# Two steps moved in a fused attention and feed-forward kernel: the last batch's state rows, and four units of the second product

## The chip, the cores and the metric

The kernel runs on one core of a Trainium2 chip. The metric is the device time of one execution in microseconds (us). A core has TensorE (PE, matmuls; its weight loads are shown as PEld), VectorE (DVE), ScalarE (ACT), GpSimd (POOL) and SyncE (SP, which here only issues DMAs). Each engine works through its own list of instructions in order, and waits for another engine by semaphores.

## The reference

Attention between 8 batches of 512 rows and 32 state rows, 8 heads of 64, in both directions, and then a two-layer network with a leaky relu over the joined 4352 rows:

```python
scores = scale * x @ state.T ; a = softmax(scores) ; xread = a @ state      # 512 rows a batch
scores2 = scale * state @ x.T ; a2 = softmax(scores2) ; sread = a2 @ x      # 32 state rows a batch
attn = concatenate([xread, sread], axis=2)                                  # (8, 8, 544, 64)
x = attn.transpose(0, 2, 1, 3).reshape(8 * 544, 512)
h = x @ w_in          # 512 -> 2048
g = maximum(0.01 * h, h)
out = g @ w_out       # 2048 -> 512
```

## The kernel before

All data are held in bf16 for the products and summed in fp32. Order within each engine is the order in which the program was written: nothing is rescheduled.

For a batch's 512 rows the first product is rearranged: xread is never formed. Instead M = state times w_in (by heads) is computed (`a_m`, matmuls at L368, into the tile `pm`), copied out of PSUM by `m_evict` or by the copies at L1188 and L1166, and h = a times M is made in 16 steps s, each of two matmuls of 512 columns into a bank `ph` (`ff1`, L389). ACT applies the leaky relu, from `ph` to `hT` (L394). There are two `ph` banks.

The second product of a batch is done by a scheme with seven products in place of eight, numbered n = 1, 2, 6, 5, 7, 3, 4, over sums of parts of h (`su`, L655) and of w_out (`tw`). It is split into units (n, m), m from 0 to 7, each of two matmuls of 256 columns into `yq` (L666). n = 1, 6, 7, 4 add into one bank, n = 2, 5, 3 into the other. After n's last unit ACT saves the bank (`sv`, L675) or DVE adds it to a saved one (`yo`, L678).

The loop over batches b = 2 to 7 has 16 steps. In each, `ff1` makes a row of h, and `fill(s)` or `units(n)` runs a number of units: first those left of the batch before, then the first 15 of this batch itself (`OWN`). How many at which step stands in `PACE`, and for batch 2, whose first ten steps are taken by the second half of batch 1's rows (`half.run(7)`), in `PACE2`. In step 10, the three column blocks of the next batch's M are computed one after the other (called M's session here): `pm0` in the PSUM tile named big, `pm1` in the one named sc (which held the scores that the exponent `a_exp2`, L287, reads), `pm2` in the two `ph` banks. Then DVE and ACT copy `pm2` (L1188), and ACT copies `pm0` (L382). Step 10's `fill` stands ahead of M's session. Step 11's stands behind it and ahead of step 11's `ff1`; from step 12 on it stands behind the step's `ff1` again.

In the last batch (b = 7) there is no next one, and steps 4 to 11 do the first product by the seven-product scheme too (`FastLast`, two halves r of seven products, L552, tile `pl`). Products 1, 6, 7, 4 of a half share one bank, 2, 5, 3 the other. ACT saves products 1, 6 and 7 (L565), DVE saves 5 (L568), and DVE joins 2 and 3 with saved ones (L571); POOL adds 7 to 5 (L574). Relus follow (L559), some of them held back until the next save (`flush`). The second half runs in steps 8 to 11: products 1 and 2, then 6 and 5, then 7 and 3, then 4, with two units behind each product (four behind product 4).

The 32 state rows of each batch are read by `a_sread_rows` for batches 0 to 6. For batch 7 `a_sread` does it: 16 matmuls of 64 columns into `psr` (L315, in the tile big), and two copies by ACT into `sr_t` (L322). `sr_t` is read by `x_sums` on DVE (L445, in step 13) and by the state rows' own first product (`FastIn`, L463), which follows the loop.

Of the kernel before, what the change touches and what calls it, by code (L numbers as in the profile page):

```python
# [27 lines left out]
def kernel(  # L28
# [68 lines left out]
    def load_x(b, eng):  # L97
        xl[b] = xpool.tile([P, H, NT * D], FP32, name="xl", tag="xl", bufs=1)
        eng.dma_start(xl[b][:], x[b].rearrange("h (p t) d -> p h (t d)", t=NT))
# [103 lines left out]
    def a_scores(a):  # L203
        sc = psum.tile([P, 2, S], FP32, name="sc", tag="sc", bufs=1)
        for k in range(NK):
            for g in range(2):
                nc.tensor.matmul(  # L207
                    sc[NS * k:NS * (k + 1), g, :],
                    lhsT=st_of(a, g, k),
                    rhs=a.xT[D * g:D * (g + 1), :, k, :],  # L210
                    start=True, stop=True,
                )
        a.sc = sc
# [46 lines left out]
    def a_shift(a, part=None):  # L260
        flat = a.sc[:].rearrange("p g c -> p (g c)")
        if part != 1:
            a.mb = block_rows(block_max(flat, NB), NB)
        if part != 0:
            a.sh = block_sub(flat, a.mb, NB)
# [38 lines left out]
    def a_a2t(a):  # L304
        a.a2T = att.tile([P, 2, NT, P], BF16, name="a2T", tag="a2T", bufs=3)
        nc.sync.dma_start_transpose(
            a.a2T[:].rearrange("p g i q -> p (g i) q"),
            (a.a2 if a.b == B - 1 else a.e2)[:].rearrange("p g s -> p (g s)"),
        )

    def a_sread(a):
        ps = psum.tile([P, NK, 2, NS], FP32, name="psr", tag="big", bufs=1)
        for k in range(NK):
            for i in range(NT):
                nc.tensor.matmul(  # L315
                    ps[:, k, :, :],
                    lhsT=a.xb[:, i, 2 * k:2 * k + 2, :].rearrange("p h d -> p (h d)"),
                    rhs=a.a2T[:, :, i, NS * k:NS * (k + 1)],
                    start=(i == 0), stop=(i == NT - 1),
                )  # L320
        for g in range(2):
            nc.scalar.copy(  # L322
                sr_t[D * g:D * (g + 1), a.b], ps[D * g:D * (g + 1), :, g, :],
            )
# [51 lines left out]
    def m_evict(a, c, pm, copy):  # L376
        cols = slice(DM * c, DM * (c + 1))
        if isinstance(pm, list):
            for g in range(2):
                copy(a.M[:, g, cols], pm[g][:])  # L380
        else:
            copy(a.M[:, :, cols], pm[:])  # L382
# [3 lines left out]
    def ff1(a, hT, j):  # L386
        ph = psum.tile([P, S], FP32, name="ph", tag="ph")
        for g in range(2):
            nc.tensor.matmul(  # L389
                ph[:], lhsT=a.M[:, g, P * j:P * (j + 1)],  # L390
                rhs=a.aT[:, g, :],
                start=(g == 0), stop=(g == 1),
            )
        nc.scalar.activation(out=hT[:, j, :], in_=ph[:], func=AF.Prelu, alpha=0.01)  # L394
# [368 lines left out]

    OWN = 15
    PACE = (1, 4, 4, 4, 3, 4, 4, 3, 4, 4, 4, 4, 3, 4, 3, 3)
    PACE2 = (0,) * 10 + (3, 3, 2, 2, 2, 3)

    att_of = [Attn() for _ in range(B)]
    a0, a1, a2 = att_of[:3]
# [290 lines left out]
    for b in range(2, B):  # L1060
        hT = hpool.tile([P, 16, S], BF16, name="hT", tag="hT")
        a = att_of[b]
        nxt = att_of[b + 1] if b + 1 < B else None
        now = Batch(b, hT)
        std = []
        if b == 2:
            std = [(i, 3) for i in range(2)]
            for n in (0, 1):
                half.f.sums(n)

        def fill(s):
            units((PACE2 if b == 2 else PACE)[s])

        def units(n):
            left = min(n, len(before.units)) if before else 0
            if left:
                before.run(left)
            if n > left:
                now.run(n - left)

        for s in range(16):
            fast = nxt is None and 4 <= s < 12
            if fast:
                n = 1 if s in (7, 11) else 2
                k = PACE[s]
                for i in range(n):
                    fl.product()
                    units((i + 1) * k // n - i * k // n)
            elif s == 11:
                fill(s)  # L1090
            if not fast:
                ff1(a, hT, 4 + s if nxt is None and s < 4 else s)
            if s == 0:
                if b + 2 < B:
                    load_x(b + 2, nc.sync)
                a_a2t(a)
                if before:
                    for n in (0, 1):
                        before.f.sums(n, 4, 8)
            elif s == 1:  # L1100
                if nxt is not None:
                    a_scores(nxt)
                m_evict(a, 3, a_m(a, 3, "big"), SCA)
                if b == 2:
                    a_sread_rows([a0])
                elif b % 2:
                    a_sread_rows([att_of[b - 2], att_of[b - 1]])
                if b == 2:
                    half.f.sums(2)
                    a_shift(nxt, 0)  # L1110
                elif nxt is not None:
                    a_shift(nxt)
                if b + 2 < B:
                    open_xb(b + 2)
                    for h in range(0, H, 2):
                        cast_x(b + 2, h, h + 2, POO)
                if before:
                    before.f.sums(2, 4, 8)
            elif s == 3:
                if before:  # L1120
                    before.f.sums(3)
                if nxt is not None and b > 2:
                    a_max2(nxt)
            elif s == 4:
                if b == 2:
                    state_t(1)
                elif b == 4:
                    sread_t(0, 3)
                elif b == 7:
                    sread_t(1, 4)  # L1130
            elif s == 8:
                if nxt is None:
                    a_sread(a)
            elif s == 12:
                for n in range(3):
                    now.f.sums(n, 0, 4)
            if nxt is None:
                if s == 1:
                    fl = FastLast(a, hT)
                    fl.sums()  # L1140
                elif s in (6, 10):
                    fi.w_sum({6: 1, 10: 3}[s])
                elif s == 13:
                    fl.flush()
                    fi.x_sums()
            elif b >= B - 3 and s == 14:
                if b == B - 3:
                    fi = FastIn(None)
                fi.w_sum(2 * (b - (B - 3)))
            if s == (9 if b == 2 else 7) and b + 2 < B:  # L1150
                a_open(att_of[b + 2], b + 2)
                a_xt_dma(att_of[b + 2])
            if nxt is not None:
                if b == 2 and s < 11:
                    if s in (8, 9):
                        a_exp2(nxt, s - 8)
                elif s == 5:
                    a_exp(nxt)
                elif s in (7, 8):
                    a_exp2(nxt, s - 7)  # L1160
                    if s == 7:
                        a_probs(nxt)
                elif s == 11:
                    a_probs2(nxt)
                elif s in (12, 13):
                    SCA(nxt.M[:, s - 12, DM:2 * DM], pm1[:, s - 12, :])  # L1166
            if std:
                i, jq = std.pop(0)
                piece(1, h1, i, jq)
            elif b == 2 and half.units:  # L1170
                half.run(7)
                if s == 4:
                    a_shift(nxt, 1)
                    half.f.sums(3)
                    weights_sum(3)
                    a_max2(nxt)
                elif s == 6:
                    a_exp(nxt)
                elif s == 8:
                    a_probs(nxt, 0)  # L1180
            elif s != 11 and not fast:
                fill(s)
            if s == 10 and nxt is not None:
                pm0 = a_m(nxt, 0, "big")
                pm1 = a_m(nxt, 1, "sc")
                pm2 = a_m(nxt, 2, "ph")
                for g, copy in enumerate((VEC, SCA)):
                    copy(nxt.M[:, g, 2 * DM:3 * DM], pm2[g][:])  # L1188
                m_evict(nxt, 0, pm0, SCA)
                if b == 2:  # L1190
                    a_probs(nxt, 1)
        before = now
# [90 lines left out]
```

## Time and profile before

| | us |
|---|---|
| median of 3 runs | 203.49 (203.1 to 204.0) |
| profiled execution, its own time | 203.36 |
| its span, first to last instruction | 201.6 |
| PE busy | 195.9 (97%) |
| DVE busy | 159.5 (79%) |
| ACT busy | 145.0 (72%) |
| POOL busy | 42.6 (21%) |

The granted TensorE clock is 1.00 over the span. Busy times on PE come from modelled ends of matmuls: consecutive matmuls overlap in the record, so small waits between them do not show as idle time there. They show in the starts, from one matmul to the next, and in the chain of waits, where a piece's length is the time until the next piece. In a timeline row the columns are start, length, engine, line, operation, out<-in and shapes, and the number of instructions merged; the brackets give idle time before it and who ended it. The rows of M's session in batch 2's stretch lie at 66.3 to 67.1 us, those of the last batch's steps 8 to 11 at 166.3 to 172.1 us.

### The profile page before, as it was taken

The page shows a single profiled execution, that of the slowest core. Times are in us where ns is not written, and L with a number is a line of the kernel's source. Part 1 is how long each engine was busy: PE and PEld are TensorE (multiplying, and loading weights), DVE is VectorE, ACT ScalarE, POOL GpSimd, SP SyncE. Part 2 cuts the span into 40 slices and gives each one's busy share as a digit, 9 for nine tenths or more (in the row PEclk, how much of TensorE's full clock was granted, in tenths as well). Part 3 has the DMA queues.
Part 4 walks back from the last instruction along what each step waited for, and adds up shares of the span by engine and source line. Part 5 has one row for each costly group of instructions (what it writes and reads, how often), then busy time and mean ns, then how long its engine had stood idle before and what let it go on. Part 6 is the DMA issues. An engine that isn't in the chain of part 4 may idle for free.

```text
span 201.6 us, 4848 instructions
## 1 busy us (share of the span) xinstructions
PE 195.9 (97%) x2000; PEld 129.2 (64%) x2000; DVE 159.5 (79%) x241; ACT 145.0 (72%) x267; POOL 42.6 (21%) x69
## 2 busy tenths in 40 slices
PE   7899999999999999999999999999999999999993
PEld 2543444444377567766776677676767688799882
DVE  1676679899989889985997599779978977995612
ACT  3459839589869886978697868787878768767710
POOL 8931002021009005200410040200020014104250
PEclk9999999999999999999999999999999999999999
DMA  6999995999794995549343945250029101310035
GB/s 198 218 206 277 232 301 99 133 311 238 131 210 127 123 282 96 104 167 274 81 78 124 281 75 99 107 156 5 0 86 173 31 3 66 142 55 3 0 90 170
DMA packets 39733, 27.99 MB, mean 139 GB/s; under 512 B 25312, under 2 KB 36704, under 8 KB 39712
## 3 DMA queue, kind: packets, MB, share of 16 engines
q1 hardware_dynamic: 34512, 20.88, 43.3%
q0 software_dynamic: 4912, 6.55, 15.9%
q10 hardware_dynamic: 288, 0.26, 0.6%
q8 instruction: 15, 0.25, 0.5%
q14 instruction: 6, 0.05, 0.1%
HBM read 17.30 MB, written 8.91 MB: 130 GB/s over the span
## 4 chain that ended last, share of the span: by engine, by line
PE 96%; DVE 1%; ACT 1%; issue 0%
PE yq L666 40%; PE ph L389 22%; PE py L596 7%; PE pm L368 4%; PE pyw L596 3%; PE pf L463 3%; PE yu L666 3%; PE pspin L132 3%; PE ph L929 2%; PE pl L552 2%; PE sc L207 1%; PE psn L333 1%; PE phw L400 1%; PE php L929 1%; DVE M L382 1%; ACT xT L791 1%
## 5 line engine op out<-in xcount | busy, mean ns | idle before, releaser
L394 ACT ACTIVATE hT<-ph 128x512 bf16<-128x512 f32 x100 | 58.9, 605 | 18.0 <-PE ph L389 17.6
L389 PE MATMUL ph<-aT,M 128*128 128x512 bf16 x200 | 57.8, 379 | 0.0
L666 PEld LDWEIGHTS <-su 128*128 128x128 bf16 x448 | 42.9, 98 | 13.8 <-DVE su L655 0.8
L666 PEld LDWEIGHTS <-hT 128*128 128x128 bf16 x312 | 30.1, 98 | 13.5 <-issue 2.0
L666 PE MATMUL yq<-tw_xf,su 128*128 128x256 bf16 x208 | 29.6, 273 | 0.0
L666 PE MATMUL yq<-w_out_bf,hT 128*128 128x256 bf16 x208 | 29.2, 273 | 0.0
L105 POOL CAST xb<-xl 128x512 bf16<-128x512 f32 (+1 forms) x21 | 14.1, 709 | 59.0 <-DMA xl<-in_x_dram 44.6
L389 PEld LDWEIGHTS <-M 128*128 128x128 bf16 x200 | 19.4, 98 | 7.3 <-issue 0.8
L655 DVE TENSOR_TENSOR su<-hT 128x1024 bf16<-128x1024 bf16 x26 | 18.1, 698 | 7.1 <-ACT hT L394 7.1
L675 ACT COPY sv<-yq 128x512 f32<-128x512 f32 (+1 forms) x28 | 15.4, 555 | 2.1 <-PE yq L666 1.4
L736 POOL TENSOR_TENSOR yo<-sv,sv 128x512 f32<-128x512 f32 x6 | 7.8, 1302 | 40.3 <-ACT sv L675 23.3
L596 PE MATMUL py<-w_out_bf,hT 128*128 128x512 bf16 x64 | 16.0, 379 | 0.0
L596 PEld LDWEIGHTS <-hT 128*128 128x128 bf16 x96 | 9.0, 98 | 10.8 <-issue 0.9
L666 PE MATMUL yq<-tw_x,su 128*128 128x256 bf16 x104 | 14.6, 273 | 0.0
L666 PE MATMUL yq<-w_out_bf,su 128*128 128x256 bf16 x104 | 14.5, 272 | 0.0
L382 ACT CAST M<-pm 128x1024 bf16<-128x1024 f32 x13 | 13.2, 1014 | 0.9 <-PE pm L368 0.9
L666 PE MATMUL yq<-tw_x,hT 128*128 128x256 bf16 x96 | 13.6, 273 | 0.0
L678 DVE TENSOR_TENSOR yo<-yq,sv 128x512 f32<-128x512 f32 x17 | 11.6, 684 | 1.5 <-PE yq L666 1.5
L287 ACT ACTIVATE e<-sc,mcols 128x512 bf16<-128x512 f32 x16 | 11.1, 697 | 0.2 <-DVE mcols L281 0.2
L279 DVE TENSOR_REDUCE mcol<-sc 128x2 f32<-128x1024 f32 x8 | 9.7, 1214 | 0.0
L655 DVE TENSOR_TENSOR su<-su,hT 128x1024 bf16<-128x1024 bf16 x13 | 9.0, 692 | 0.4
L217 DVE TRANSPOSE_TENSOR_REDUCE mrow<-sc 128x32 f32<-128x1024 f32 x7 | 8.7, 1244 | 0.6 <-PE sc L207 0.5
(167 smaller groups left out, 295.7 us busy)
## 6 DMA issues: line engine op xcount, KB each, us to landing
xl<-in_x_dram SPq DMA_DIRECT2D x5, 1024.0 KB, 6.6
out_dram<-yo SPq DMA_DIRECT2D x10, 512.0 KB, 2.7
w_in_bf<-in_moe_w_in_dram POOLq DMA_DIRECT2D x4, 512.0 KB, 9.2
w_out_bf<-in_moe_w_out_dram POOLq DMA_DIRECT2D x4, 512.0 KB, 17.0
out_dram<-ysb SPq DMA_DIRECT2D x8, 256.0 KB, 6.6
xf<-in_x_dram SPq DMA_DIRECT2D x2, 512.0 KB, 4.8
x<-in_x_dram POOLq DMA_DIRECT2D x2, 512.0 KB, 14.0
xl<-in_x_dram POOLq DMA_DIRECT2D x1, 1024.0 KB, 19.4
```

The lines of the kernel that those rows point to most:

```text
L105: copy(xs[b][:, :, h0:h1].rearrange("p t h d -> p h t d"), xl[b][:, h0:h1].rearrange("p h (t d) -> p h t d", t=NT),)
L217: nc.vector.tensor_reduce(out=m1[:], in_=flat.rearrange("p (c j) -> p c j", j=NS), axis=AX.X, op=ALU.max, apply_transpose=True,)
L279: nc.vector.tensor_reduce(out=m2[:], in_=a.sc[:], axis=AX.X, op=ALU.max, negate=True)
L287: nc.scalar.activation(out=a.e2[:, g], in_=a.sc[:, g, :], func=AF.Exp, bias=a.m2s[:, g:g + 1], scale=SCALE, accum_out=a.r2[:, g:g + 1],)
L382: copy(a.M[:, :, cols], pm[:])
L389: nc.tensor.matmul(ph[:], lhsT=a.M[:, g, P * j:P * (j + 1)], rhs=a.aT[:, g, :], start=(g == 0), stop=(g == 1),)
L394: nc.scalar.activation(out=hT[:, j, :], in_=ph[:], func=AF.Prelu, alpha=0.01)
L596: nc.tensor.matmul(y.py, lhsT=hT[:, j, P * i:P * (i + 1)], rhs=w_out_bf[:, j, :], start=(j == 0), stop=(j == 15),)
L655: (eng or nc.vector).tensor_tensor(out=S[n][:, ms], in0=u[:, ms], in1=v[:, ms], op=op)
L666: nc.tensor.matmul(bank[:, i, :], lhsT=lhs[:, m, P * i:P * (i + 1)], rhs=rhs[:, m, :], start=(first and m == 0 and (i == 0 or of is not No ...
L675: copy(t[:], bank)
L678: nc.vector.tensor_tensor(out=dst, in0=bank, in1=self.sv[n][:], op=ALU.add)
```

## The change

Two edits. In the last batch, `a_sread` is called in step 11, behind the product and the units of that step, in place of step 8, behind that step's products and units. And `PACE2` gives 1, 4, 3, 3, 2, 2 units to batch 2's steps 10 to 15 in place of 3, 3, 2, 2, 2, 3: two units (four matmuls) fewer stand ahead of M's session in step 10, four units in place of three stand directly behind it, and the sum stays 15.

```diff
     OWN = 15
     PACE = (1, 4, 4, 4, 3, 4, 4, 3, 4, 4, 4, 4, 3, 4, 3, 3)
-    PACE2 = (0,) * 10 + (3, 3, 2, 2, 2, 3)
+    PACE2 = (0,) * 10 + (1, 4, 3, 3, 2, 2)
...
                 elif b == 7:
                     sread_t(1, 4)
-            elif s == 8:
-                if nxt is None:
-                    a_sread(a)
             elif s == 12:
                 for n in range(3):
                     now.f.sums(n, 0, 4)
...
                 elif s in (6, 10):
                     fi.w_sum({6: 1, 10: 3}[s])
+                elif s == 11:
+                    a_sread(a)
                 elif s == 13:
                     fl.flush()
                     fi.x_sums()
```

In the built program, PE's order and ACT's change (the two copies at L322 move from behind the save of product 1 to behind the last relus of `FastLast` that precede step 12's). DVE, POOL and SP have the same instructions in the same order. Line numbers of the changed kernel are one lower from there on.

## The prediction

> **What bounds the kernel now.** I read the page's busy times first, then the chain of waits in order of time, then the timelines of ACT, DVE and PE around the two edits.
>
> ```profile
> PE 195.9 (97%) x2000; PEld 129.2 (64%) x2000; DVE 159.5 (79%) x241; ACT 145.0 (72%) x267; POOL 42.6 (21%) x69
> ```
>
> TensorE (PE) sets the time, and the page gives it 96% of the chain. Neither edit adds or removes a matmul, so only PE's small waits can change. Start to start, a matmul of 256 columns takes 109 ns and one of 512 columns 216 ns when nothing is waited for; anything longer is a wait. Batch 2's stretch, from the chain:
>
> ```profile
> 67.19 0.76 PE yq L666 x6
> 67.95 1.00 PE ph L389 x4
> ...
> 69.38 0.55 PE ph L389 x2
> ...
> 70.36 0.43 PE ph L389 x2
> ```
>
> Four ph matmuls are worth 0.86 us and two 0.43, so 1.00 and 0.55 hide waits. From the starts one by one they are 136 ns (ff1 of step 11 starts at 67.920, 51 ns after ACT's M copy at L1188 ends at 67.869) and 120 ns (ff1 of step 13 starts at 69.336, 51 ns after step 11's relu ends at 69.285). The six yq matmuls ahead are too short a cover for the eviction of M. What stands ahead of M's session:
>
> ```profile
> 65.40 0.69 ACT L287 ACTIVATE e<-sc,mcols 128x512 bf16<-128x512 f32 x1
> ...
> 66.06 0.61 ACT L394 ACTIVATE hT<-ph 128x512 bf16<-128x512 f32 x1
> 67.28 0.59 ACT L1188 CAST M<-pm 128x512 bf16<-128x512 f32 x1 [0.61 <-PE pm L368]
> ```
>
> ACT runs without a break until step 10's relu ends at 66.672; only then does it idle 0.61 us, until M's matmuls are done. The last batch, steps 8 to 11:
>
> ```profile
> 167.83 0.47 PE psr L315 x16
> ...
> 168.96 0.22 PE pl L552 x2
> ...
> 169.61 0.35 PE pl L552 x2
> ...
> 170.40 0.32 PE pl L552 x2
> ```
>
> Two pl matmuls are worth 0.22 us, so products 7 and 3 of FastLast's second half wait 138 and 102 ns. Product 7 needs product 6 saved by ACT, product 3 needs product 5 saved by DVE:
>
> ```profile
> 166.40 0.62 ACT L559 ACTIVATE hT<-ls 128x512 bf16<-128x512 f32 x1
> 166.92 0.58 ACT L675 COPY sv<-yq 128x512 f32<-128x512 f32 x1
> 167.38 0.60 ACT L565 COPY ls<-pl 128x512 f32<-128x512 f32 x1
> ...
> 168.40 0.53 ACT L322 CAST sr_t<-psr 64x128 bf16<-64x128 f32 x2
> 168.95 0.59 ACT L565 COPY ls<-pl 128x512 f32<-128x512 f32 x1
> ```
> ```profile
> 168.02 0.69 DVE L571 TENSOR_TENSOR ls<-pl,ls 128x512 f32<-128x512 f32 x1 [0.26 <-ACT ls L565]
> 168.99 0.69 DVE L678 TENSOR_TENSOR yo<-yq,sv 128x512 f32<-128x512 f32 x1 [0.28 <-PE yq L666]
> 169.60 0.68 DVE L568 COPY ls<-pl 128x512 f32<-128x512 f32 x1
> ```
>
> The save of product 1 ends at 167.985, behind three other ACT instructions; the 16 psr matmuls (16 x 29 ns = 0.465 us) cover it. The two sr_t copies stand ahead of the save of product 6. PE goes on 51 ns after ACT and 54 ns after DVE is done, here and above; I use these.
>
> **Part one: units in batch 2.** PACE2 gives 1, 4, 3, 3, 2, 2 units at steps 10 to 15 for 3, 3, 2, 2, 2, 3: 15 either way, two matmuls each. Ahead of M's 24 matmuls stand 2 yq matmuls for 6, behind them 8 for 6. No DMA is issued by these units, and SP's and POOL's orders stay. M's session is three blocks of eight matmuls; the last one takes both ph banks, and one of them is still read by step 10's relu: its second matmul waits for ACT in both built orders.
>
> - Four matmuls less: M's session could start 4 x 109 = 436 ns sooner, at 65.909. Its middle block (sc bank) needs the exponent done, 66.185 + 0.051 = 66.24. Its last block needs the relu: 66.672 + 0.051 = 66.723 for that second matmul, against 66.790 now. So the session ends about 66 ns sooner, not 436: a new wait of 370 ns. The relu can't come sooner: ACT is back to back from 64.245, when DVE's mcols releases it, and nothing ahead of that moves.
> - Behind: the yq matmuls start at 67.053 and eight take 119 + 7 x 109 = 0.88 us, to 67.937. ACT's M copy, 66 ns sooner too, ends at 67.803 and allows 67.854, so the 136 ns go. Step 13's ff1 comes after two ff1 (0.86) and six yq (0.655), at 69.453; step 11's relu allows about 69.27, so the 120 ns go.
> - Units done by then: 8 in both. So +370 - 136 - 120 = +114 ns; directly, 69.453 - 69.336 = **+0.117 us**. I take 0.12.
> - Nothing later absorbs it: the next batches' starts show no wait over 0.03 us beside fixed costs of changing between kinds of matmul. Tightest is the unit of h row 15 in batch 3's step 0: PE at 72.71, relu about 72.65. A miss would cost under 0.1 us.
>
> Bounds: -0.256 us (both old waits go, no new one) to +0.22 us (miss included).
>
> **Part two: state rows of batch 7.** The 16 matmuls and two ACT copies move from behind step 8 to behind step 11. No DMA moves.
>
> - Product 6 stands next in line at 167.671, 0.465 us sooner. But it adds into the bank that product 1's save still reads: 167.985 + 0.051 = 168.036. New wait 365 ns. All ACT work ahead of that save belongs to earlier steps, so it stays put.
> - Product 5 would start at 168.692 but needs DVE's L571, which itself waits for the same save and ends at 168.709: 168.763, a wait of 71 ns.
> - Without the sr_t copies, product 6's save ends near 169.05; product 7 comes at 169.418, without wait: the 138 ns go.
> - Product 3 needs product 5's save, behind DVE's yo sum, which needs the yq matmuls 0.10 us sooner than now: L568 ends at 170.182, product 3 at 170.236, its wait 163 ns for 102.
> - Sum of waits 365 + 71 + 163 = 599 against 240 ns: **+0.36 us**. Directly: product 4 at 170.89, the eight yq done at 171.98, psr 0.465, so step 12's ff1 at 172.447 against 172.079, +0.37. I take 0.36.
> - Later: the copies run 172.71 to 173.23, and step 12's relu is 0.07 us late for it; ff1 of step 14, first to want that bank, comes at 174.8. DVE's x_sums read sr_t at 175.46, 2.2 us after. Both hidden; if that cover were gone, up to the copies' 0.53 us.
>
> Bounds: -0.24 us (both waits go, no new one) to +0.89 (copies exposed as well).
>
> **Sum.** +0.12 + 0.36 = +0.48 us. The profiled execution took 203.36 us (span 201.6 and 1.8 around it): 203.84. The median of the runs is 0.13 higher: 203.97, so 204.0. About 0.5%, 1.0 us, is what a measurement of this kernel can tell from no change; the forecast lies within.
>
> **Rivals.**
> - *It works as free order (faster):* M's session and product 6 go ahead as soon as their matmuls are next, and all four old waits go: -0.256 - 0.240 = -0.50 us, 203.0. For it: the waits named are real, and batches 3 to 6, with eight matmuls behind M, show none there. Against: both releases come from ACT, whose times above are fixed by earlier work, and the two waits stand in the built order. 0.10.
> - *Only one wait bites:* +0.12 - 0.24 or -0.256 + 0.36, that is 203.4 or 203.6. Needs step 10's relu, or product 1's save, over 0.3 us sooner than recorded. 0.08.
> - *Slower, by the clock:* two new pauses of 0.37 us could lower the granted clock. Price: in the opening a 512-column matmul took 427 ns instead of 216, over at least 5.6 us (1.2 to 6.8); one such episode later loses half of that, 2.8 us: 206.8. It decides if pauses of 0.37 us are enough. Against: 437 ns between two starts at 12.4 us and 267 ns of pause at 20.0 us were followed by matmuls at 216 ns, with a granted clock of 1.00 over the span. 0.06. The Trainium skill ("TensorE: Matmul & The Clock Gate", Part 1) puts the idle window that halves the clock at about 3.4 us, by which this rival dies; in the same part it says that short pauses between groups of matmuls, as banks are cycled, made the clock oscillate in one kernel, by which it could live. By the first the sum stays; the trace's pauses at full clock agree with the first.
> - *The moves change nothing:* excluded as to order; as to time it would need the waits to cancel within 0.1 us, part of the second rival.
>
> **How the numbers follow.** Forecast 0.76, free order 0.10, one wait 0.08, clock 0.06. The runs before lie between 203.1 and 204.0, -0.4 to +0.5 around their median; around 203.97 that is 203.6 to 204.5. Down to the free order's upper half, and up by part two's exposed copies, gives 203.2 to 204.9, which leaves out the clock and part of the free order. Slower by over 0.5% (above 204.5): about a quarter of the forecast's chance, through spread and unseen knock-ons, and the clock: 0.24. Faster by over 0.5% (below 202.5): a part of the free order, 0.04. The rest, 0.72, within.
>
> **What would show it.** After: in the M session a gap of about 0.37 us ahead of M's last block, with step 10's relu ending just before it; ff1 of steps 11 and 13 without wait; step 13's ff1 0.12 us later than before. In batch 7, product 6 starting 0.05 us after product 1's save, waits at products 5 and 3, none at 7, and step 12's ff1 0.37 us later relative to product 1. No gap ahead of M's last block or product 6, or a granted clock under 1.00, proves me wrong.

## The result and the profile after

The changed kernel takes 203.79 us (median of 22 runs, 203.37 to 204.22) against 203.39 us (202.85 to 204.0) for the kernel before, measured beside it: a ratio of 1.002, 95% interval 1.0012 to 1.0028, that is +0.24 to +0.57 us. The profiled execution took 204.18 us, with a span of 202.4. The page of the changed kernel:

```profile
PE 194.0 (96%) x1976; PEld 128.6 (64%) x2000; DVE 158.5 (78%) x241; ACT 145.1 (72%) x267; POOL 42.7 (21%) x69
```

24 of the 2000 matmul records are missing in this trace, and as many in each of the later ones, so stretches are measured here by PE's 2000 weight loads, which are all there. M's session of batch 2, PE's timeline of the changed kernel:

```profile
65.52 0.38 PE L666 MATMUL yq<-w_out_bf,hT 128*128 128x256 bf16 x2
65.83 0.41 PE L368 MATMUL pm<-w_in_bf,st_t 64*32 64x512 bf16 x8
66.55 0.89 PE L368 MATMUL pm<-w_in_bf,st_t 64*32 64x512 bf16 x16 [0.31 <-ACT e L287]
67.38 1.05 PE L666 MATMUL yq<-w_out_bf,hT 128*128 128x256 bf16 x8
```

Before, the 24 matmuls of M ran as one row. Now eight run, PE waits, and the other sixteen follow: the middle block starts 0.72 us after the first, where 0.23 would be free of waits. ACT's timeline of the same kernel says for what:

```profile
64.57 0.69 ACT L287 ACTIVATE e<-sc,mcols 128x512 bf16<-128x512 f32 x1 [0.56 <-DVE mcols L281]
...
66.29 0.21 ACT L287 ACTIVATION_READ_ACCUMULATOR e<-sc,mcols 128x1 f32 x1
66.38 0.60 ACT L394 ACTIVATE hT<-ph 128x512 bf16<-128x512 f32 x1
67.53 0.59 ACT L1187 CAST M<-pm 128x512 bf16<-128x512 f32 x1 [0.54 <-PE pm L368]
```

The exponent ends at 66.50 and step 10's relu at 66.99; the middle block goes on 51 ns after the one, and the second matmul of the last block 51 ns after the other. That makes two waits, 0.50 us ahead of the middle block and 0.27 us ahead of the last, in place of the one of 0.37 us that was forecast. The first row holds the reason: ACT waited 0.56 us for mcols, against 0.17 before:

```profile
64.25 0.69 ACT L287 ACTIVATE e<-sc,mcols 128x512 bf16<-128x512 f32 x1 [0.17 <-DVE mcols L281]
```

The last batch, chain of waits of the changed kernel:

```profile
168.49 0.38 PE pl L552 x2
...
169.30 0.29 PE pl L552 x2
...
170.03 0.22 PE pl L552 x2
...
170.68 0.38 PE pl L552 x2
...
172.59 0.47 PE psr L315 x16
```

Product 6 opens a stretch of PE behind ACT's save in this chain; product 5 is 0.07 us over the 0.22 that two pl matmuls are worth, product 7 is free of wait, product 3 is 0.16 over, and psr comes last. ACT's timeline there:

```profile
167.84 0.60 ACT L565 COPY ls<-pl 128x512 f32<-128x512 f32 x1
168.31 0.65 ACT L559 ACTIVATE hT<-ls 128x512 bf16<-128x512 f32 x1
168.90 0.59 ACT L565 COPY ls<-pl 128x512 f32<-128x512 f32 x1
```

Product 1's save ends at 168.436 and product 6 starts at 168.487, 51 ns behind it. The sr_t copies have left the place ahead of the second save.

### The profile page after: what moved, and what is told of

It reads as the page before. It is cut to its first block, busy times and chain, and to the rows that moved or that the text cites. A ratio compares the mean times of both kernels' runs of the same rounds, so it can differ in the third digit from the quotient of the medians.

```text
span 202.4 us, 4825 instructions
## 1 busy us (share of the span) xinstructions
PE 194.0 (96%) x1976; PEld 128.6 (64%) x2000; DVE 158.5 (78%) x241; ACT 145.1 (72%) x267; POOL 42.7 (21%) x69
## 4 chain that ended last, share of the span: by engine, by line
PE 85%; DMA 5%; DVE 4%; ACT 2%; POOL 2%; issue 1%; POOLq 0%; DVEq 0%
PE yq L666 37%; PE ph L389 19%; PE py L596 7%; DMA w_in_bf<-in_moe_w_in_dram 5%; PE pm L368 4%; PE pyw L596 3%; PE pf L463 3%; PE yu L666 3%; PE ph L929 2%; PE pl L552 2%; PE sc L207 1%; PE psn L333 1%; PE phw L400 1%; POOL w_in_bf L118 1%; DVE tw_x L632 1%
## 5 line engine op out<-in xcount | busy, mean ns | idle before, releaser
L389 PE MATMUL ph<-aT,M 128*128 128x512 bf16 x183 | 54.9, 379 | 0.3
L655 DVE TENSOR_TENSOR su<-hT 128x1024 bf16<-128x1024 bf16 x26 | 17.8, 683 | 8.1 <-ACT hT L394 8.1
L655 DVE TENSOR_TENSOR su<-su,hT 128x1024 bf16<-128x1024 bf16 x13 | 9.0, 692 | 0.4
```

What stands on the lines that cost most here:

```text
L389: nc.tensor.matmul(ph[:], lhsT=a.M[:, g, P * j:P * (j + 1)], rhs=a.aT[:, g, :], start=(g == 0), stop=(g == 1),)
L655: (eng or nc.vector).tensor_tensor(out=S[n][:, ms], in0=u[:, ms], in1=v[:, ms], op=op)
```

## The experiments

A whole run's time here carries noise that the change has no part in, so each run is read twice: by the ratio of its runs to the kernel before on the same chip, and in its trace by stretches, as the shift of the same weight loads against the profiled execution of before. The stretches run to batch 2's step 9, from there to batch 3's step 1, on to batch 7's step 8, from there to step 12, and to the end. The column mcols is the end of DVE's mcols less the start of PE's weight load at the end of the first stretch: how late the max is for PE.

| kernel | to batch 2 | batch 2 | middle | batch 7 | rest | mcols |
|---|---|---|---|---|---|---|
| before | 0 | 0 | 0 | 0 | 0 | -0.19 |
| after | -0.08 | **+0.525** | 0.00 | **+0.362** | 0.00 | +0.21 |
| pace_only | -0.52 | **-0.146** | 0.00 | 0.00 | 0.00 | -0.81 |
| sread_only | -0.02 | 0.00 | +0.04 | **+0.361** | 0.00 | -0.19 |
| pace_cover | -0.20 | **-0.037** | 0.00 | 0.00 | 0.00 | -0.19 |
| sread_hold | -0.56 | 0.00 | +0.03 | **0.000** | 0.00 | -0.60 |
| early_old | -0.09 | 0.000 | 0.00 | 0.00 | 0.00 | -0.88 |
| early_new | -0.30 | **-0.146** | 0.00 | 0.00 | 0.00 | -0.88 |
| tail_fix | +0.23 | 0.00 | 0.00 | **-0.230** | **+0.186** | -0.19 |
| both | -0.47 | **+0.325** | 0.00 | **-0.229** | **+0.183** | +0.01 |
| late_old | -0.46 | **+0.948** | 0.00 | 0.00 | 0.00 | +0.83 |
| late_new | -0.57 | **+0.890** | 0.00 | 0.00 | 0.00 | +0.57 |
| tail_fix2 | -0.66 | **+0.135** | 0.00 | **-0.230** | 0.00 | +0.01 |
| both2 | -0.09 | **-0.146** | 0.00 | **-0.230** | 0.00 | -0.88 |

The first stretch moves between -0.66 (tail_fix2) and +0.23 us (tail_fix), although neither of these two kernels has an edit in it; only the early load (four kernels) and the doubled sum (two) lie there. This is noise that whole times carry.

**Each part alone.** pace_only is the kernel before with the new PACE2; sread_only is the kernel before with a_sread in step 11.

> The kernel before with the new PACE2 alone. Theory (a new wait ahead of M's last block takes the place of the two old ones): the session ends at most 0.07 us sooner although 0.44 us of matmuls were taken from ahead of it; steps 11 and 13 no longer wait; 0.0 to +0.2 us against before, depending on how late the exponent's max comes from DVE in the run; in the trace a gap between M's first and last block that ends 0.05 us after the relu of step 10 or the exponent. Rival (free order): -0.26 us and no gap. Rival (all of the change's loss is here): +0.40 us.

Measured: ratio 1.0006 (0.9995 to 1.0017); in the trace batch 2's stretch is 0.146 us *shorter*. In this execution mcols came 0.6 us sooner than before, and of the gap in M's session 0.09 us was left, ahead of the last block; steps 11 and 13 no longer wait. The runs' +0.12 us lies in what the theory expected, the trace outside it, between the theory and the free order.

> The kernel before with the state rows' read in step 11 alone. Theory (the 16 matmuls covered the save of product 1): product 6 starts 0.05 us after that save, waits of about 0.37, 0.07 and 0.16 us at products 6, 5 and 3, +0.36 us against before. Rival (free order): -0.24 us. Rival (all of the loss is in batch 2): 0.0 us.

Measured: ratio 1.0023 (1.0012 to 1.0035), trace +0.361 us, waits of 367, 76 and 162 ns at products 6, 5 and 3. The theory holds; the rivals fall. Most of the change's loss is here.

**The save that holds product 6.** sread_hold is sread_only with one relu moved behind the save:

```diff
             elif n == 4:
                 relu(1, 0, flat)
-                self.flush()
+                if r: self.flush()
                 self.late.append((relu, 1, 1, sv[5]))
```

> sread_only, with one of the relus that FastLast holds back (product 3 of the first half) done behind the save of the second half's product 1 in place of ahead of it, so that this save ends about 0.5 us sooner. Theory (that save releases product 6): product 6 starts without wait; waits of about 0.14 us at product 5 and 0.10 at product 3 stay, by DVE; 0.0 us against before, -0.36 against sread_only. Rival (product 6 is held by something else): +0.36 us against before, as sread_only.

Measured: ratio 1.0006 (0.9996 to 1.0016), and 0.000 in the trace. ACT's timeline of sread_hold, where the order relu, sv, save now reads sv, save, relus:

```profile
165.87 0.58 ACT L675 COPY sv<-yq 128x512 f32<-128x512 f32 x1
166.33 0.60 ACT L565 COPY ls<-pl 128x512 f32<-128x512 f32 x1
166.81 1.17 ACT L559 ACTIVATE hT<-ls 128x512 bf16<-128x512 f32 x2
```

and its chain of waits, products 6, 5 and 3:

```profile
167.30 0.22 PE pl L552 x2
...
167.95 0.30 PE pl L552 x2
...
169.35 0.36 PE pl L552 x2
```

Product 6 is at its free length, products 5 and 3 wait 0.09 and 0.15. One relu moved out of the way of that save gives the trace's 0.36 us back, with psr still in step 11: the save was the cause.

**More cover behind M.** pace_cover is the kernel before with PACE2 3, 4, 3, 2, 2, 1.

> The kernel before with PACE2 3, 4, 3, 2, 2, 1: the three units ahead of M's session stay, and four and three stand behind it. Theory (the units ahead cover step 10's relu, the units behind cover M's eviction, and both covers are wanted): no new gap in the session, no wait at steps 11 and 13, -0.25 us up to where ACT's relus are late at steps 14 and 15; -0.25 to -0.10 us in all. Rival (ACT sets the pace of the whole stretch, and the place of units is without effect): within 0.05 us of before. Rival (the units behind are what costs): as pace_only.

Measured: ratio 1.0005 (0.9995 to 1.0014), trace -0.037 us. The session has no gap and steps 11 and 13 don't wait, as expected; but the chain of waits of pace_cover has two pairs of yq matmuls that are 0.10 longer than their 0.22:

```profile
71.65 0.33 PE yq L666 x2
...
72.42 0.32 PE yq L666 x2
```

They wait for ACT, for the relus of the rows of h that they read (102 and 90 ns). Of the 256 ns that were saved, 192 came back there. The size expected was wrong, and -0.037 us is what the first rival gave; but its reason does not hold, for the place of the units had the effect that the theory named, and the gain was lost further on. From its copy of M on, ACT works without a break until the relu of the first of these waits ends. Ahead of the second relu ACT had been idle for 0.15 us: there the two ff1 matmuls and one unit that PE has in between are a shorter cover than the relu.

**How late mcols come.** In the changed kernel's own execution, batch 2's stretch was 0.525 us longer, not 0.12. DVE's timelines, before:

```profile
60.37 0.68 DVE L655 TENSOR_TENSOR su<-hT,su 128x1024 bf16<-128x1024 bf16 x1
60.97 1.63 DVE L632 TENSOR_TENSOR tw_x<-tw_xf,w_out_bf 128x2048 bf16<-128x2048 bf16 x1
...
63.77 0.45 DVE L281 TENSOR_SCALAR mcols<-mcol 128x2 f32<-128x2 f32 x1
```

and after:

```profile
60.29 1.07 DVE L655 TENSOR_TENSOR su<-hT,su 128x1024 bf16<-128x1024 bf16 x1
61.29 1.62 DVE L632 TENSOR_TENSOR tw_x<-tw_xf,w_out_bf 128x2048 bf16<-128x2048 bf16 x1
...
64.08 0.45 DVE L281 TENSOR_SCALAR mcols<-mcol 128x2 f32<-128x2 f32 x1
```

The same sum took 1.07 us in place of 0.68, and mcols ended that much later. POOL's casts of batch 4's x, before and after:

```profile
60.76 3.43 POOL L105 CAST xb<-xl 128x512 bf16<-128x512 f32 x4 [14.43 <-ACT sv L675]
```
```profile
60.21 3.74 POOL L105 CAST xb<-xl 128x512 bf16<-128x512 f32 x4 [13.68 <-DMA xl<-in_x_dram]
```

After, the casts started 0.08 us ahead of the sum; before, 0.39 us behind its start. When they start hangs on the landing of the load of x: in all ten traces with the load in its old place the first cast starts 0.15 us behind the landing, which lies anywhere from 58.1 to 61.7 us (60.61 before, where the row names ACT instead; 60.06 after). early_old and early_new issue that load sooner, with the old and the new PACE2:

```diff
+        if s == 9:
+            load_x(4, nc.sync)
         if s in (5, 9):
             load_state(1, range(s // 2 - 2, s // 2))
...
-                if b + 2 < B:
+                if 2 < b < B - 2:
                     load_x(b + 2, nc.sync)
```

> The kernel before, with the load of batch 4's x issued some 3 us sooner (in step 9 of batch 1's loop), so that POOL's casts of it no longer fall on DVE's two bf16 sums ahead of the max; units as before. Theory (the old PACE2 keeps M's session behind the relu in any case): DVE's mcols end some 0.4 us or more sooner against PE, and nothing is gained: within 0.1 us of before. Rival (the casts cost something by themselves): faster by over 0.2 us.

> The same earlier load with the changed PACE2; the state rows' read as before. Theory (what part one costs is how late mcols and so step 10's relu are): no wait over 0.1 us ahead of M's last block, and -0.15 us against before and against early_old; the sign of part one turns. Rival (part one costs the same whenever mcols come): +0.1 us against early_old, with a gap of 0.37 us or more in M's session.

Measured: early_old 0.9996 (0.9983 to 1.0008), trace 0.000; early_new 0.9986 (0.9974 to 0.9998), trace -0.146 us. In both, DVE's L632 took 1.22 us where it takes 1.63 in the execution before, and L281 0.17 where it takes 0.45; mcols ended 0.69 us sooner against PE. PE's timeline of early_new has M's session in one row again, now behind two units fewer; a wait of 0.09 us ahead of its last block is left within the row:

```profile
65.30 0.38 PE L666 MATMUL yq<-w_out_bf,hT 128*128 128x256 bf16 x2
65.61 0.94 PE L368 MATMUL pm<-w_in_bf,st_t 64*32 64x512 bf16 x24
66.48 1.05 PE L666 MATMUL yq<-w_out_bf,hT 128*128 128x256 bf16 x8
```

So part one's sign turns with mcols, and the earlier mcols alone bring nothing. This is what the traces say; the ratios of the two kernels overlap. late_old and late_new do the sum at L655 twice, which makes mcols late:

```diff
-                    half.f.sums(3)
+                    half.f.sums(3); half.f.sums(3)
                     weights_sum(3)
```

> The kernel before with one of DVE's sums ahead of the max (half.f.sums(3)) done twice, so that mcols end about 0.7 us later against PE; old PACE2. Theory (everything ahead of M's last block hangs on mcols, exponent, relu, with slope one): with the old PACE2 the slack is 0.07 us, so a gap of about 0.6 us opens in M's session, and +0.6 us against before. Rival (lateness of DVE is absorbed by PE's units): 0.0 us.

> The same doubled sum with the changed PACE2. Theory: both PACE2 are held up at the same place, so the new one loses only the units that it has to make up behind (0.44 us less the two old waits of 0.26): gap of about 1.05 us in the session, +0.8 us against before, +0.2 against late_old. Rival (the new PACE2's cost grows with lateness without end): +1.1 us or more against before.

Measured: late_old 1.0036 (1.002 to 1.0052), late_new 1.0052 (1.0031 to 1.0072); traces +0.948 and +0.890 us, with mcols at +0.83 and +0.57. The rival of late_old (0.0 us) falls by the runs as well, that of late_new (+1.1 us or more) by the trace alone. PE's timeline of late_old shows the same gap with the old PACE2:

```profile
65.89 0.41 PE L368 MATMUL pm<-w_in_bf,st_t 64*32 64x512 bf16 x8
66.79 0.90 PE L368 MATMUL pm<-w_in_bf,st_t 64*32 64x512 bf16 x16 [0.49 <-ACT e L287]
```

All traces but pace_cover's, which has a PACE2 of its own, lie on two lines. With x for the column mcols, batch 2's stretch costs the larger of 0 and x + 0.12 with the old PACE2, and the larger of -0.146 and x + 0.316 with the new: at x = +0.01 the old gives 0.135 measured and 0.13 by the line, at +0.83 0.948 and 0.95; the new at +0.01 0.325 and 0.33, at +0.21 0.525 and 0.52, at +0.57 0.890 and 0.89. The slope is one, as expected. Late mcols hold both, and then by these lines the new one loses 0.20 us against the old; that late_new's trace lies below late_old's is because its mcols came 0.25 us sooner.

**The two old waits of the last batch.** tail_fix leaves psr in step 8 and moves what stood ahead of the two saves. Of its edit this is the part that sets the new places, the two sr_t copies behind product 6 (i = 0) and the yo sum of n = 3 with its store behind product 5; the rest splits `a_sread` and holds that sum back:

```diff
                     fl.product()
+                    if s == 9:
+                        if i == 0:
+                            a_sread_out(a)
+                            before.held = []
+                        else:
+                            for f, *args in before.held:
+                                f(*args)
                     units((i + 1) * k // n - i * k // n)
```

> The kernel before with the state rows' 16 matmuls left in step 8, their two ACT copies moved behind the save of product 6 (step 9), and DVE's yo sum of the batch before moved behind the save of product 5. Theory (the two old waits are two queues: ACT's copies ahead of one save, DVE's sum ahead of the other): no wait at products 6, 5, 7, 3; -0.24 us against before. Rival (moving matmuls is what counts, the queues do not): 0.0 us.

Measured: ratio 0.9995 (0.9982 to 1.0008), which can't tell theory from rival. The trace has the gain, -0.230 us, with no wait at products 6, 5, 7 and 3, and then +0.186 us back in step 13, where yq matmuls wait for DVE. DVE's timeline before and of tail_fix:

```profile
171.43 1.58 DVE L433 TENSOR_TENSOR sw<-w_in_bf,sw 128x2048 bf16<-128x2048 bf16 x1
```
```profile
171.43 1.92 DVE L435 TENSOR_TENSOR sw<-w_in_bf,sw 128x2048 bf16<-128x2048 bf16 x1
173.28 0.68 DVE L680 TENSOR_TENSOR yo<-yq,sv 128x512 f32<-128x512 f32 x1
```

The yo sum that frees the bank stands behind a sum of w_in that took 1.92 us (1.58 before). That sum ends 1.08 us behind the end of POOL's sum at L574 in both traces, and POOL's came 0.34 us later in tail_fix, since ACT's save of product 7, which it reads, now stands behind the moved sr_t copies. both adds the early load and the new PACE2 to tail_fix:

> early_new and tail_fix together. Theory: the gains add, -0.39 us against before. Rival (PE's time is given back later, to ACT's relus or to the last stores): at most the larger of the two, -0.24 us.

Measured: 0.9991 (0.9978 to 1.0004). In this execution the casts of x were just over, but POOL's next cast, of state rows, started 0.06 us ahead of DVE's sum in spite of the early load; the sum took 1.10 us, mcols came later than before, and batch 2's stretch cost +0.325. The last batch gave -0.229 and then +0.183 back, as in tail_fix, so neither gain was kept. tail_fix2 and both2 move w_sum(3) from step 10 to step 11, behind that yo sum:

> tail_fix with DVE's long sum of w_in (w_sum(3)) moved behind the yo sum that PE waited for in step 13. Theory (tail_fix's gain was given back at that wait): batch 7's steps 8 to 11 0.23 us shorter as in tail_fix, no wait of 0.19 us after them, -0.23 us against before. Rival (DVE is full there and the wait moves on to x_sums or the sums of h): the 0.19 us come back by the first state rows' product or the units of n = 6.

> tail_fix2 with the earlier load and the changed PACE2. Theory: -0.23 from the last batch and -0.15 (casts clear of DVE's sums) to +0.33 us (one collision, as in the run of both) from batch 2: -0.38 us against before where the casts stay clear. Rival: gains don't add, -0.15 us at most.

Measured: tail_fix2 0.9982 (0.9972 to 0.9991), both2 0.9978 (0.9967 to 0.9989). In both traces the 0.230 us stay. The chain of waits of both2, products 6, 5, 7 and 3, all at their free length:

```profile
168.07 0.22 PE pl L554 x2
...
168.72 0.22 PE pl L554 x2
...
169.38 0.22 PE pl L554 x2
...
170.03 0.22 PE pl L554 x2
```

Both are faster than the kernel before, by about 0.2%, and so than the changed one; between the two the intervals don't decide. In tail_fix2 the rival falls: the 0.19 us do not come back.

## Why the prediction was right

- **The sum and the side.** +0.48 us was forecast, +0.40 us measured (0.24 to 0.57), within 0.5% as forecast. The closeness is owed to part two; what part one adds over many executions is known only as -0.10 to +0.35 us (pace_only), and that its share fits is in part luck.
- **Part two, 0.36 us.** Measured 0.362 and 0.361. The three new waits were 366, 74 and 164 ns in the changed kernel, forecast 365, 71 and 163; the old wait at product 7 went. sread_hold shows the cause of the first: without it, the loss is gone. The two edits' later costs, forecast as hidden, were: the rest of the span shows 0.00.
- **Part one, 0.12 us.** The mechanism was right: the 436 ns taken from ahead of M came back as a wait for ACT, and steps 11 and 13 no longer wait. By the line above, the new PACE2 costs +0.12 us at the mcols of before's profile, as forecast; this is read off the line, for no trace with the new PACE2 had its mcols there. But the step that took the relu's end as fixed, since nothing ahead of it moves, failed: nothing moves in the order, yet DVE's mcols came between 0.62 us sooner (pace_only) and 0.40 us later (the changed kernel) against PE in executions of kernels that touch neither the load nor DVE's sums. Step 10's relu and the wait moved with them: 0.77 us of wait in the session for the 0.37 forecast. The bound of +0.22 us missed the 0.525 of the changed kernel's profile; set against an old PACE2 equally late, the excess is 0.20. A bound by this row should have carried the spread of DVE's sums, as seen over several traces.
- **The rivals.** Free order is out for part two, and for part one where mcols are late; where they are early it is nearly what happens (-0.146 of -0.256). So the rival that only one wait bites was the state of some executions. The clock rival is out: in late_new two matmuls of M's session start 1.06 us apart, where 0.20 would be free of waits, and the matmuls of 512 columns behind them still take 216 ns. The starts show this; the granted clock alone, which the prediction took as a sign, would not do, for the profile gives it as 1.00 also for 1.2 to 6.8 us, where a matmul of 512 columns took 427 ns.

## What to carry to other kernels

Matmuls ahead of a step may be covering a wait of that step: before moving them away, ask what releases each of its operands and banks, and how much earlier that can be. A margin of 0.07 us read from one execution is not a margin when the releasing chain goes through an engine whose same instruction takes 0.68 us in one execution and 1.07 in the next; compare that chain in several traces. And when a wait is removed, ask which queue comes next: tail_fix lost most of its gain to DVE's, pace_cover to ACT's relus.

## What the runs showed of the hardware

DVE and POOL hold each other up, and which of them is held up hangs on who starts first. DVE's bf16 sum of 128x1024 at L655, with both inputs in SBUF, took 0.67 to 0.69 us in all 14 traces wherever no POOL instruction was running when it began. With a cast of POOL's running it took up to 1.10 us, and each of the 14 sums so lengthened ended 0.54 us behind the end of that cast. The other way round, POOL's cast took 0.61 us alone and up to 1.66, and one that began within such a sum, or within that of 128x2048, ended 0.47 us behind it. The sum of 128x2048 at L632 took 1.22 us, or 1.63 with a cast running when it began. Even the small instruction at L281, 0.17 us alone, ended 0.02 us behind a POOL instruction in ten of the traces. The Trainium skill ("SBUF — State Buffer", Who interferes with whom) says that a DVE instruction with two SBUF inputs and a GpSimd instruction that reads SBUF shut each other out for the whole instruction, by order of issue. The durations agree with it; no run here shows the port itself. With the new PACE2, such a collision of 0.4 us reached PE in full, by way of mcols, exponent and relu; other sums that were lengthened alike, in batch 3's stretch at 78 us, cost PE nothing (the column middle).
